# One more PSUM snapshot a unit, the output product one and a half units late, turned tiles fetched a phase ahead, norms and splits dealt out by a plan

## The chip, the cores and the metric

The kernel runs on one core of one Trainium2 chip. The metric is device time of one execution in microseconds (us), lower is better. TensorE (PE) multiplies matrices into PSUM; VectorE (DVE), ScalarE (ACT) and GpSimd (POOL) do elementwise work; SyncE (SP) issues all DMAs of this kernel. Each engine runs its own instructions in the order in which they are written.

## The reference

```python
scores = (1/S) * z @ z.T                  # per batch: B = 4, S = 3008, d_qk = 64
out    = u * (relu(scores) ** 2 @ v)      # v, u: 3008 x 256
x      = out.reshape(12032, 256)
xn     = x / sqrt(mean(x * x, -1) + 1e-6) * rms_g
g, val = xn @ w_gate, xn @ w_val          # 256 x 1536 each
result = (g * sigmoid(g) * val) @ w_out   # 1536 x 256
```

## The kernel before

Everything is kept transposed (features on partitions, tokens on columns). Each float32 matrix is split into a high and a low part, and a product is made of three matmuls (high by high, low by high, high by low).

The tokens are worked on in twelve pairs p of two column blocks of 512 (480 in every third pair), three pairs to a batch of 3008. Stage A(p) is attention for pair p: 24 steps ("slots") over key blocks of 128. A step takes scores (`emit_s`, PE lines 352 and 353, then ACT relu, line 357, and a DVE product, 359), splits them (`emit_l`: ACT 375, DVE 378, and ACT 395 or DVE 393 where a copy, "halves", is kept in DRAM), and multiplies them with v (`emit_av`: PE 417, 418, 422). Scores are symmetric, so some tiles are not computed again but fetched turned from those copies (`load_turned`, tile T). After the last step `emit_gate` (440) multiplies with u.

Stage M(p) is the feed-forward part: twelve units f of 128 hidden features (`Unit.run`). A unit forms its two 2x2 block products by Winograd's scheme, with seven products (A11, A12, S1, S2, S3, A22, S4; PE 597 to 599) into three PSUM tiles X, Z and V. X grows by five products; ACT copies it out in between (603: the snapshots s1, s2, s3), and DVE combines: 673 (Z + s1), 689 (V + s3), 692 (X * s1), 645 (V + s2), 652 (s2 * s3), with two Silus on ACT (682, 649). The two results of a unit are split (ACT 608 high, DVE 613 low: hH, hL) and multiplied with w_out (`y(0)`, `y(1)`: PE 624, 625, 628). In line 689 V is read in PSUM before its last product S4 is added, so S4 follows 689.

The stages stand in the order A0, A1, M0, A2, M1, ... A11, M10, M11. At the end of an M stage `tail` finishes its last unit while the next A stage enters. Four PSUM banks serve X, Z, V and the score tiles in rotation.

A table `jobs` holds side work at (stage, slot): `hook(phase, slot)` runs it in place. A unit has three slots: 3f behind y(0), 3f+1 behind y(1), 3f+2 ahead of A22. Side work is the norm of the next pair (`norm_jobs`: squares, sums, a 32x32 transpose, a fold matmul, an inverse root in small steps, scaling, four differences), the splits of keys (`prep_stat`) and of v (`prep_v`) for the next batch in M1, M4 and M7, the splits of the next queries (`prep_mov`, mh and ml), and in A0, A1 and M0 the decoding of the weights. `spread` deals it evenly over slots.

Of the kernel before, what the change touches and what calls it, by code (L numbers as in the profile page):

```python
# [19 lines left out]
P = 128  # L20
CH = 512
# [9 lines left out]
def kernel(  # L31
# [197 lines left out]
    raws = {True: ["raw", "xl4", "raw", "xl5", "xl6"], False: ["raw"]}  # L229

    def new_raw(first):
        ring = raws[first]
        ring.append(ring.pop(0))
        t = ring[-1]
        return (work if t == "raw" else moving).tile([P, CH], F32, tag=t, name="raw", bufs=2 if t == "raw" else 1)

    def prep_mov(p, k):
# [5 lines left out]
        def load():  # L243
            raw = tiles["raw"] = new_raw(p == 0)
            nc.sync.dma_start(out=raw[:, :n], in_=zT2[:, t0 + k * CH:t0 + k * CH + n])
# [12 lines left out]
    def prep_stat(b, c, shared=None):  # L258
# [6 lines left out]
        def load():  # L265
            raw = tiles["raw"] = new_raw(b == 0)
# [4 lines left out]
        def split():  # L271
            raw = tiles["raw"]
            z = keep.tile([P, CH], F32R, tag=f"zst{c}", name=f"zst{c}")
            nc.scalar.copy(z[:, :m], raw[:, :m])
            nc.vector.tensor_tensor(z[lo, :m], raw[lo, :m], f32(z[lo, :m]), op=ALU.subtract)
            zst[b, c] = z

        return load, split

    def prep_v(b, g):  # L280
# [4 lines left out]
        def load():  # L285
            view = tiles["raw"] = new_raw(b == 0).rearrange("p (a d) -> p a d", a=2)
# [7 lines left out]
        def split():  # L294
            hi = vh[b, g] = keep.tile([P, 2, D], F32R, tag=f"vh{g}", name=f"vh{g}")
            nc.scalar.copy(hi, tiles["raw"])
            lo = vl[b, g] = keep.tile([P, 2, D], F32R, tag=f"vl{g}", name=f"vl{g}")
            nc.vector.tensor_tensor(lo, tiles["raw"], f32(hi), op=ALU.subtract)

        return load, split  # L300
# [249 lines left out]
    def split_jobs(p):  # L550
# [3 lines left out]
        def one(o):  # L554
            def go():
# [8 lines left out]
                nc.vector.tensor_tensor(lo[:, :n], val, f32(hi[:, :n]), op=ALU.subtract)  # L564
                xsplit[p, o] = (hi, lo)
            return go
# [5 lines left out]
    units = {}  # L572

# [14 lines left out]
    class Unit:  # L588
# [12 lines left out]
        def snap(self, ps):  # L601
            s = work.tile([P, CH], F32, tag="r", name="s", bufs=6)[:, :self.n]
            nc.scalar.copy(s, ps[:, :self.n])  # L603
# [47 lines left out]
        def end2(self):  # L651
            nc.vector.tensor_tensor(self.s2, self.s2, self.s3, op=ALU.mult)

        def end3(self):
            self.high(1, self.s2)

        def end4(self):
            self.low(1, self.s2)

        def run(self, phase, prev, fill_a, fill_b):  # L660
# [10 lines left out]
            if prev:  # L671
                prev.end2()
            nc.vector.tensor_tensor(self.s1, Z[:, :n], self.s1, op=ALU.add)
            if prev:
                prev.end3()
# [12 lines left out]
            hook(phase, 3 * f + 1)  # L688
            nc.vector.tensor_tensor(self.s3, V[:, :n], self.s3, op=ALU.add)  # L689
# [4 lines left out]
            if f + ahead(self.p) < NF:  # L694
                load_unit(self.p, f + ahead(self.p))

        def tail(self, fills):

            fills = iter(fills)

            def fill():
                fn = next(fills, None)
                if fn:
                    fn()

            self.end0()
            fill()
            self.end1()
            self.end2()
            self.end3()  # L710
            self.y(0)
            fill()
            self.end4()
            self.y(1)

    def phase_a(p):

        ph = ("A", p)
        for i in range(NK):
# [5 lines left out]
            if i < NK - 1:  # L725
                for k in range(2):
                    emit_av(p, i, k)

    def rest_a(p):
        def one(k):  # L730
# [4 lines left out]
        return one(0), one(1)  # L735
# [4 lines left out]
    def phase_m(p, prev, fills):  # L740
        ph = ("M", p)
        for f in range(NF):
            u = Unit(p, f)
            if f == 0 and fills:
                a, b = fills
            else:
                a, b = (lambda u=prev: u.y(0)), (lambda u=prev: u.y(1))
            u.run(ph, prev, a, b)
# [5 lines left out]
    def spread(phase, slots, fns):  # L754
        slots = list(slots)
        for i, fn in enumerate(fns):
            at(phase, slots[min(i * len(slots) // len(fns), len(slots) - 1)], fn)

    def plan_batch(b):

        phase = ("M", b * NP - 2)
        todo = [prep_stat(b, c) for c in range(NC)] + [prep_v(b, g) for g in range(NK // 2)]
        return phase, todo

    for p in range(NPAIR):
        b, c0 = where(p)[:2]
        ph = ("A", p)
        if p:

            before = ("M", p - 2) if p > 1 else ("A", 0)  # L770
            for k in range(2):
                load, split, _ = prep_mov(p, k)
                if p > 1:
                    at(before, 3 * 9 + 2, load)
                    at(before, 3 * 10 + k, split)
                else:
                    at(before, NK - 4, load)
                    at(before, NK - 1, split)
        if p == 1:
            spread(ph, range(1, 18), [lambda i=i: deque(norms(0)[i]() or (), maxlen=0) and None for i in range(23)])  # L780
        if p:
            jl = [lambda i=i, p=p: splits(p - 1)[i]() for i in range(NO)]
            spread(ph, range(19, 23) if p == 1 else range(0, 7), jl)
        at(ph, 1 if p == 0 else (23 if p == 1 else 9), lambda p=p: load_u(p))
        for i in range(0, NK, 2):
            for k in range(2):
                if is_turned(p, i, k):
                    at(ph, max(i - 6, 0), lambda p=p, i=i, k=k: load_turned(p, i, k))
        for f in range(ahead(p - 1)):
            if p:  # L790
                at(ph, NK - 3 + f, lambda p=p, f=f: load_unit(p - 1, f))
        m = ("M", p - 1)
        if p:
            spread(m, range(1, 28) if p < NPAIR - 1 else range(1, 24), [lambda p=p, i=i: norms(p)[i]() for i in range(23)])
        if p == NPAIR - 1:
            spread(m, range(24, 36), [lambda p=p, i=i: splits(p)[i]() for i in range(NO)])
# [11 lines left out]

    for b in range(1, batch):
        phase, todo = plan_batch(b)  # L810
        n = len(todo)
        for k, (load, split) in enumerate(todo):
            s = 1 + 30 * k // n
            at(phase, max(s - 3, 0), load)
            at(phase, s + 1, split)
# [9 lines left out]
    for c in range(2, NC):  # L825
        s = 4 * c - 4
        at(("A", 0), s - 3, first["z", c][0])
        at(("A", 0), s, first["z", c][1])
    for g in range(2, NK // 2):
        s = 2 * g - 2  # L830
        at(("A", 0), max(s - 2, 0), first["v", g][0])
        at(("A", 0), s, first["v", g][1])
# [33 lines left out]
    with tc.manual_schedule():  # L866
# [6 lines left out]
        for c in range(2):  # L873
            first["z", c][1]()
            first["m", c][1]()
            if c == 0:
                first["v", 0][1]()
        emit_s(0, 0)
        first["v", 1][1]()
        emit_s(0, 1)  # L880
        emit_l(0, 0)
        phase_a(0)

        for go in rest_a(0):
            go()
        for go in enter_a(1):
            go()
        phase_a(1)
        fills = rest_a(1)
        prev = None  # L890
        for p in range(NPAIR):
            prev = phase_m(p, prev if not fills else None, fills)
# [43 lines left out]
```

## Time and profile before

| | |
|---|---|
| time, median of 3 runs | 2234.55 us (2229.3 to 2235.33) |
| time of the profiled execution | 2229.75 us |
| span of the profiled execution | 2228.0 us |
| PE busy | 2087.1 us (94%) |
| DVE busy | 1643.3 us (74%) |
| ACT busy | 1366.8 us (61%) |
| POOL busy | 129.1 us (6%) |
| mean granted TensorE clock | 0.978 |

The time is taken around the execution, the span from its first to its last instruction. A busy PE holds overlapping matmuls: the 512 column matmul is listed with about 390 ns, but the next one starts 227 ns later.

### The profile page before, as it was taken

How to read it: one execution, taken by the hardware profiler on the slowest of the kernel's cores; microseconds unless marked ns; L12 is line 12 of the kernel's file. 1: busy time of each engine (PE TensorE's matmuls, PEld its weight loads, DVE VectorE, ACT ScalarE, POOL GpSimd, SP SyncE). 2: the span in 40 equal slices, each digit the busy share in tenths (PEclk: the TensorE clock that was granted, in tenths of full speed). 3: DMA queues.
4: the chain of work that ended last, by engine and by line, in shares of the span. 5: the costliest groups of instructions: out<-in, count | busy, mean ns of one | idle time of the engine just before them, and what ended most of it. 6: DMA issues, size and time to landing. Idle time of an engine off the chain costs nothing. (4 is left out here: it accounts for less than half of the span.)

```text
span 2228.0 us, 26491 instructions
## 1 busy us (share of the span) xinstructions
PE 2087.1 (94%) x8968; PEld 1687.8 (76%) x8968; DVE 1643.3 (74%) x2697; ACT 1366.8 (61%) x2429; POOL 129.1 (6%) x232
## 2 busy tenths in 40 slices
PE   8988789998999999998999999999899999999998
PEld 6767567766887877876778777786688877878887
DVE  8988857686877677577778658758787866875865
ACT  7777447555855855555775675645586567564554
POOL 0635520000000000000000000000000000000000
PEclk9999989999999999999999999999999999999999
DMA  3405533242532742944253553394335355366342
GB/s 129 147 5 158 160 111 103 79 151 78 190 133 92 184 138 85 206 148 141 95 184 126 127 170 116 105 208 148 101 147 161 109 141 163 125 132 163 118 149 86
DMA packets 306825, 295.81 MB, mean 133 GB/s; under 512 B 195200, under 2 KB 232192, under 8 KB 306688
## 3 DMA queue, kind: packets, MB, share of 16 engines
q1 hardware_dynamic: 306688, 294.12, 43.9%
q8 instruction: 70, 1.15, 0.2%
q14 instruction: 67, 0.55, 0.1%
HBM read 178.46 MB, written 69.47 MB: 111 GB/s over the span
## 5 line engine op out<-in xcount | busy, mean ns | idle before, releaser
L597 PE MATMUL ps<-xh,wu 128*128 128x512 f32 (+1 forms) x1008 | 406.7, 404 | 61.0 <-DVE s L689 51.2
L417 PE MATMUL po<-H,vh 128*128 128x512 f32 (+1 forms) x1152 | 453.3, 394 | 9.2 <-ACT H L375 5.6
L418 PE MATMUL po<-H,vl 128*128 128x512 f32 (+1 forms) x1152 | 450.3, 391 | 0.0
L608 ACT CAST hH<-s 128x512 fp32r<-128x512 f32 (+1 forms) x288 | 176.4, 612 | 440.7 <-DVE s L692 324.7
L598 PE MATMUL ps<-xh,wu 128*128 128x512 f32 (+1 forms) x1008 | 394.2, 391 | 3.2 <-DMA wu<-wc 3.2
L599 PE MATMUL ps<-xl,wu 128*128 128x512 f32 (+1 forms) x1008 | 393.6, 391 | 0.0
L603 ACT COPY s<-ps 128x512 f32<-128x512 f32 (+1 forms) x432 | 248.6, 575 | 155.1 <-PE ps L599 147.0
L422 PE MATMUL po<-L,vh 128*128 128x512 f32 (+1 forms) x1104 | 340.6, 390 | 1.6 <-DVE L L378 1.3
L359 DVE TENSOR_TENSOR r<-ps,r 128x512 f32<-128x512 f32 x356 | 230.8, 680 | 123.0 <-ACT r L357 122.7
L597 PEld LDWEIGHTS ps<-xh,wu 128*128 128x128 f32 x1008 | 191.7, 190 | 147.6 <-DVE s L689 75.2
L357 ACT ACTIVATE r<-ps 128x512 f32<-128x512 f32 (+1 forms) x392 | 215.9, 599 | 133.8 <-PE ps L353 121.2
L378 DVE TENSOR_TENSOR L<-r,H 128x512 fp32r<-128x512 f32 x368 | 252.7, 697 | 49.4 <-ACT H L375 43.2
L417 PEld LDWEIGHTS po<-H,vh 128*128 128x128 f32 x1152 | 220.8, 192 | 59.0 <-ACT H L375 10.0
L418 PEld LDWEIGHTS po<-H,vl 128*128 128x128 f32 x1152 | 220.6, 192 | 41.9
L422 PEld LDWEIGHTS po<-L,vh 128*128 128x128 f32 x1104 | 209.2, 190 | 45.2 <-DVE L L378 5.3
L624 PE MATMUL py<-hH,woh 128*128 128x512 f32 (+1 forms) x576 | 224.7, 390 | 1.1 <-ACT hH L608 1.1
L628 PE MATMUL py<-hL,woh 128*128 128x512 f32 (+1 forms) x576 | 181.1, 396 | 46.0 <-DVE hL L613 46.0
L625 PE MATMUL py<-hH,wol 128*128 128x512 f32 (+1 forms) x576 | 223.2, 388 | 0.0
L599 PEld LDWEIGHTS ps<-xl,wu 128*128 128x128 f32 x1008 | 191.8, 190 | 38.4
L375 ACT CAST H<-r 128x512 fp32r<-128x512 f32 x356 | 217.8, 628 | 0.9 <-DVE r L359 0.9
L598 PEld LDWEIGHTS ps<-xh,wu 128*128 128x128 f32 x1008 | 192.1, 191 | 33.1 <-DMA wu<-wc 4.2
L613 DVE TENSOR_TENSOR hL<-s,hH 128x512 fp32r<-128x512 f32 (+1 forms) x288 | 196.4, 682 | 24.1 <-ACT hH L608 8.4
(80 smaller groups left out, 2635.8 us busy)
## 6 DMA issues: line engine op xcount, KB each, us to landing
wu<-wc SPq DMA_DIRECT2D x288, 448.0 KB, 4.0
kept<-halves SPq DMA_DIRECT2D x168, 256.0 KB, 2.0
raw<-in_v SPq DMA_DIRECT2D x44, 256.0 KB, 2.7
raw<-in_zT SPq DMA_DIRECT2D x38, 256.0 KB, 3.9
ux<-in_uT SPq DMA_DIRECT2D x16, 512.0 KB, 4.7
out_T<-y SPq DMA_DIRECT2D x32, 256.0 KB, 2.0
wc<-wohi SPq DMA_DIRECT2D x21, 256.0 KB, 2.5
wc<-wolo SPq DMA_DIRECT2D x21, 256.0 KB, 2.3
```

The source lines that it names most:

```text
L359: nc.vector.tensor_tensor(a[:, :n], ps[:, :n], a[:, :n], op=ALU.mult)
L375: nc.scalar.copy(hi[:, :n], a[:, :n])
L378: nc.vector.tensor_tensor(lo[:, :n], a[:, :n], f32(hi[:, :n]), op=ALU.subtract)
L417: nc.tensor.matmul(po[d][:, :n], wh[:, j, ds], hi[:, :n], start=(i == 0), stop=False)
L418: nc.tensor.matmul(po[d][:, :n], wl[:, j, ds], hi[:, :n], start=False, stop=(ends and lo is None))
L422: nc.tensor.matmul(po[d][:, :n], wh[:, j, ds], lo[:, :n], start=False, stop=ends)
L597: nc.tensor.matmul(ps[:, :n], wh[:, o, :], xh[:, :n], start=start, stop=False, skip_group_check=True)
L598: nc.tensor.matmul(ps[:, :n], wl[:, o, :], xh[:, :n], start=False, stop=False, skip_group_check=True)
L599: nc.tensor.matmul(ps[:, :n], wh[:, o, :], xl[:, :n], start=False, stop=stop, skip_group_check=True)
L603: nc.scalar.copy(s, ps[:, :self.n])
L624: nc.tensor.matmul(acc[h, d][:, :n], woh[:, f, ds], hi[:, :n], start=(f == 0), stop=False)
L625: nc.tensor.matmul(acc[h, d][:, :n], wol[:, f, ds], hi[:, :n], start=False, stop=False)
```

## The change

In each unit, ACT copies V into a fourth snapshot s4 right after S1 and S2, and the sum of line 689 is taken from s3 and s4, both in SBUF; S4 then no longer follows that sum. The output products are kept in a queue `pend`, from which a unit takes two: y(0) of a unit is issued in the second place of the next unit, y(1) in the first place of the one after. The last one and a half steps of attention go through the same queue. The tail issues three output products instead of two, and the split of the second result (`end3`) stands behind `emit_s(1)` and `emit_l(0)` without the copies of y(0) between.

Side work is dealt by `Beside.put`: each job has an engine and a cost, each slot has room (DVE 0.75 in every slot, ACT 1.35 in each third slot 3f+2), and a job goes to the first slot with room. Splits are parted into their ACT half (`one`) and their DVE half (`two`). The v splits of the later batches have their low part on POOL, in four pieces of 128 columns. The raw tiles of these batches take six buffers in turn: two named raw, and mh0, ml0, mh1, ml1, which are also the buffers of the next queries. Turned tiles of steps 4 to 7 are fetched in the last two units of the M stage before.

```diff
+    raws = {
+        "start": ["raw", "xl4", "raw", "xl5", "xl6"],
+        "batch": ["raw", "mh0", "raw", "ml0", "mh1", "ml1"],
+        "queries": ["raw"],
+    }
...
+        def one():
             hi = vh[b, g] = keep.tile([P, 2, D], F32R, tag=f"vh{g}", name=f"vh{g}")
             nc.scalar.copy(hi, tiles["raw"])
+        def two():
...
+            for a in range(2):
+                for k in range(0, D, PIECE):
+                    c = slice(k, k + PIECE)
+                    nc.gpsimd.tensor_tensor(lo[:, a, c], tiles["raw"][:, a, c], f32(hi[:, a, c]), op=ALU.subtract)
...
-        def run(self, phase, prev, fill_a, fill_b):
+        def run(self, phase, prev):
...
             self.product(X, S2, False, False)
+            s4 = self.snap(V, later=True)
             self.s2 = self.snap(X)
             if prev:
-                prev.end4()
-            nc.scalar.activation(self.s1, self.s1, AF.Silu)
-            fill_a()
+                prev.end2()
+            nc.scalar.copy(s4, V[:, :n])
             hook(phase, 3 * f)
+            if prev:
+                prev.end3()
+            pend.popleft()()
             self.product(X, S3, False, False)
             self.s3 = self.snap(X)
-            fill_b()
+            nc.scalar.activation(self.s1, self.s1, AF.Silu)
             hook(phase, 3 * f + 1)
-            nc.vector.tensor_tensor(self.s3, V[:, :n], self.s3, op=ALU.add)
+            nc.vector.tensor_tensor(self.s3, self.s3, s4, op=ALU.add)
+            pend.popleft()()
             hook(phase, 3 * f + 2)
...
+            pend.extend([lambda: self.y(0), lambda: self.y(1)])
...
+    for i, (e, cost, gap, fn) in enumerate(norm_plan(0)):
+        at(("A", 1), 1 + i * 17 // 23 + (2 if i >= 8 else 0) - (1 if i < 8 else 0), fn)
...
+                at(m.phase, 3 * 9 + 1 + k, load)
+                at(m.phase, 3 * 10 + 2 + k, split)
```

Three places show what the order becomes. In stage A1, on PE, the fold matmul of the first norm stands before the products of one key block (vh_126 and vh_215 are the v tiles of two key blocks that follow each other). Before:

```order
L352 MATMUL ps<-mh,zst_108 128x512
L353 MATMUL ps<-ml,zst_108 128x512
L480 MATMUL ps<-misc,fold_sb 128x32
L417 MATMUL po<-H,vh_126 128x512
L418 MATMUL po<-H,vl_128 128x512
```

and now:

```order
L366 MATMUL ps<-mh,zst_108 128x512
L367 MATMUL ps<-ml,zst_108 128x512
L494 MATMUL ps<-misc,fold_sb 128x32
L431 MATMUL po<-H,vh_215 128x512
L432 MATMUL po<-H,vl_250 128x512
```

It moved two steps later on PE; the DVE sum that it reads (474, now 488) stands one slot earlier.

In the tail from M6 to A8, on DVE, from the sum V + s2 of the last unit to the copies of its output (line 645 is now 665, 613 is 633, 378 is 392). Before:

```order
L645 TENSOR_TENSOR s<-ps,s 128x512
L359 TENSOR_TENSOR r<-ps,r 128x512
L359 TENSOR_TENSOR r<-ps,r 128x448
L613 TENSOR_TENSOR hL<-s,hH 128x512
L652 TENSOR_TENSOR s<-s 128x512
L636 COPY y<-py 128x512
L359 TENSOR_TENSOR r<-ps,r 128x512
L359 TENSOR_TENSOR r<-ps,r 128x448
L378 TENSOR_TENSOR L<-r,H 128x512
L378 TENSOR_TENSOR L<-r,H 128x448
L613 TENSOR_TENSOR hL<-s,hH 128x512
L636 COPY y<-py 128x512
```

and now:

```order
L665 TENSOR_TENSOR s<-ps,s 128x512
L373 TENSOR_TENSOR r<-ps,r 128x512
L373 TENSOR_TENSOR r<-ps,r 128x448
L633 TENSOR_TENSOR hL<-s,hH 128x512
L672 TENSOR_TENSOR s<-s 128x512
L373 TENSOR_TENSOR r<-ps,r 128x512
L373 TENSOR_TENSOR r<-ps,r 128x448
L392 TENSOR_TENSOR L<-r,H 128x512
L392 TENSOR_TENSOR L<-r,H 128x448
L633 TENSOR_TENSOR hL<-s,hH 128x512
L656 COPY y<-py 128x512 x2
```

The first copy of an output went behind the second hL; the second hL still follows both L.

At the end of M1 (M4 and M7 alike), on DVE, with the second block of the next queries. Raw tile 4727 is the v block 11; it, and ml_4879, lie in the buffer ml1. Before:

```order
L250 TENSOR_SCALAR mh_4775<-raw_4709 128x512
L251 SCALAR_TENSOR_TENSOR ml_4776<-raw_4709,mh_4775 128x512
L689 TENSOR_TENSOR s_4767<-ps_4738,s_4767 128x512
L692 TENSOR_TENSOR s_4725<-ps_4718,s_4725 128x512
L645 TENSOR_TENSOR s_4745<-ps_4738,s_4745 128x512
```

and now (the first block, into mh0 and ml0, stands one unit earlier, right ahead of that unit's L710):

```order
L254 TENSOR_SCALAR mh_4878<-raw_4745 128x512
L255 SCALAR_TENSOR_TENSOR ml_4879<-raw_4745,mh_4878 128x512
L633 TENSOR_TENSOR hL_4882<-s_4779,hH_4863 128x512
L545 TENSOR_TENSOR xc_4896<-ux1_3612,xc_4866 128x480
L706 TENSOR_TENSOR s_4893<-s_4893,s_4859 128x512
L545 TENSOR_TENSOR ux0_3610<-ux1_3612,ux0_3610 128x480
L545 TENSOR_TENSOR xc_4906<-ux1_3612,xc_4896 128x480
L710 TENSOR_TENSOR s_4842<-ps_4835,s_4842 128x512
```

while POOL's queue ends with the v blocks 9, 10 and 11, whose raw tiles lie in ml0, mh1 and ml1:

```order
L312 TENSOR_TENSOR vl7_4787<-raw_4547,vh7_4741 128x128 x4
L312 TENSOR_TENSOR vl8_4792<-raw_4549,vh8_4743 128x128 x4
L312 TENSOR_TENSOR vl9_4868<-raw_4637,vh9_4820 128x128 x4
L312 TENSOR_TENSOR vl10_4873<-raw_4639,vh10_4822 128x128 x4
L312 TENSOR_TENSOR vl11_4910<-raw_4727,vh11_4908 128x128 x4
```

The query splits, which waited for their own load, now also stand behind POOL's reading of these tiles; block 11 is copied by ACT in the last slot of the stage.

## Rows read from the trace of the kernel before

**Rows 1.** Waits of PE over the span: us in total, times, longest.

```profile
PE ps L597 <- DVE s L689: 51.2, 45, 3.4
PE py L628 <- DVE hL L613: 46.0, 20, 3.5
PE ps L480 <- issue: 6.8, 1, 6.8
```

**Rows 2.** Waits of PE within M0 alone (204 to 332 us).

```profile
PE ps L597 <- DVE s L689: 14.8, 8, 2.9
```

**Rows 3.** Windows M0, M3, A8, M7: us; busy PE, PEld, DVE, ACT, POOL; clock; DMA.

```profile
204.00:332.00 128.00, 102.75 (x398) 78.49 (x397) 92.85 (x155) 57.68 (x103) 47.73 (x92) 0.89 0.44 140
792.00:884.00 92.00, 90.93 (x400) 73.81 (x399) 71.06 (x118) 48.26 (x86) 0.00 (x0) 1.00 0.29 99
1425.00:1498.00 73.00, 68.51 (x307) 58.28 (x306) 44.82 (x73) 41.66 (x76) 0.00 (x0) 0.98 0.87 193
1498.00:1606.00 108.00, 98.41 (x402) 73.89 (x401) 79.92 (x135) 56.57 (x103) 0.00 (x0) 0.98 0.39 130
```

**Rows 4.** Timeline of PE in the tail of M6: start, us, [idle before].

```profile
1424.72 0.39 PE L352 MATMUL ps<-mh,zst 128*128 128x512 f32 x1
1424.95 0.39 PE L353 MATMUL ps<-ml,zst 128*128 128x512 f32 x1
...
1427.99 0.73 PE L628 MATMUL py<-hL,woh 128*128 128x512 f32 x2 [1.15 <-DVE hL L613]
...
1433.84 0.73 PE L628 MATMUL py<-hL,woh 128*128 128x512 f32 x2 [3.33 <-DVE hL L613]
```

**Rows 5.** Timeline of ACT in the same tail.

```profile
1428.58 0.62 ACT L608 CAST hH<-s 128x512 fp32r<-128x512 f32 x1 [1.54 <-DVE s L652]
1429.10 0.58 ACT L634 COPY y<-py 128x512 f32<-128x512 f32 x1
...
1431.00 1.06 ACT L395 COPY halves<-r 128x1024 uint16<-128x1024 uint16 x1
1431.94 0.58 ACT L375 CAST H<-r 128x448 fp32r<-128x448 f32 x1
```

**Rows 6.** Timeline of DVE in the same tail.

```profile
1424.24 0.69 DVE L692 TENSOR_TENSOR s<-ps,s 128x512 f32<-128x512 f32 x1 [0.68 <-PE ps L599]
...
1433.10 0.68 DVE L613 TENSOR_TENSOR hL<-s,hH 128x512 fp32r<-128x512 f32 x1
```

**Rows 7.** End of M7: DVE, then PE.

```profile
1594.40 0.43 DVE L250 TENSOR_SCALAR mh<-raw 128x512 fp32r<-128x512 f32 x1 [2.05 <-DMA raw<-in_zT]
...
1596.21 0.80 PE L597 MATMUL ps<-xh,wu 128*128 128x512 f32 x1 [3.17 <-DVE s L689]
```

**Rows 8.** The first fold in A1: PE, then DVE.

```profile
136.19 0.60 PE L480 MATMUL ps<-misc,fold_sb 128*128 128x32 f32 x2 [6.84 <-issue]
...
135.41 0.67 DVE L474 TENSOR_REDUCE misc<-q 128x16 f32<-128x512 f32 x1
```

**Rows 9.** DVE at the end of A1, and POOL there and in M0.

```profile
190.22 1.83 DVE L564 TENSOR_TENSOR xl<-ux,xh 128x512 fp32r<-128x512 f32 x2
194.55 1.28 DVE L564 TENSOR_TENSOR xl<-xc,xh 128x512 fp32r<-128x512 f32 x2
...
188.37 3.13 POOL L124 TENSOR_TENSOR wolo<-w,wohi 128x128 fp32r<-128x128 f32 x4
275.25 1.69 POOL L124 TENSOR_TENSOR ws<-w,w 128x128 f32<-128x128 f32 x4
```

**Rows 10.** Windows after a stall: the tail of M6, and M0 at 262.8 us.

```profile
1436.00:1440.00 4.00, 4.00 (x14) 3.31 (x13) 2.75 (x5) 2.53 (x5) 0.00 (x0) 0.66 0.63 212
...
262.00:266.00 4.00, 3.23 (x14) 2.68 (x15) 3.74 (x7) 1.64 (x3) 3.92 (x8) 1.00 0.44 131
```

**Rows 11.** First unit of M7 on PE, and a small norm step on DVE.

```profile
1506.14 0.50 PE L597 MATMUL ps<-xh,wu 128*128 128x512 f32 x1 [0.95 <-DVE s L689]
...
1539.62 0.18 DVE L490 TENSOR_TENSOR misc<-misc 128x30 f32<-128x30 f32 x1
```

More of the change, by code (lines that the diff above doesn't have):

```diff
@@ L265, in load @@
         def load():
-            raw = tiles["raw"] = new_raw(b == 0)
+            raw = tiles["raw"] = new_raw("batch" if b else "start")
             nc.sync.dma_start(out=raw[:, :n], in_=zT2[:, b * S + t0:b * S + t0 + n])
@@ L269, in load @@
                 nc.sync.dma_start(out=raw[:, n:m], in_=zT2[:, (b + 1) * S - TAIL:(b + 1) * S])
[L271 to L274, printed above, removed]
+        def one():
+            z = zst[b, c] = keep.tile([P, CH], F32R, tag=f"zst{c}", name=f"zst{c}")
+            nc.scalar.copy(z[:, :m], tiles["raw"][:, :m])
+        def two():
+            raw, z = tiles["raw"], zst[b, c]
             nc.vector.tensor_tensor(z[lo, :m], raw[lo, :m], f32(z[lo, :m]), op=ALU.subtract)
-            zst[b, c] = z
-        return load, split
+        return load, one, two
     def prep_v(b, g):
@@ L285, in load @@
         def load():
-            view = tiles["raw"] = new_raw(b == 0).rearrange("p (a d) -> p a d", a=2)
+            view = tiles["raw"] = new_raw("batch" if b else "start").rearrange("p (a d) -> p a d", a=2)
             if k0 + 2 < NK:
@@ L554, in one, with high @@
         def one(o):
-            def go():
+            def high():
                 val = xsplit[p, "values"][o]
@@ L724, in phase_a, with last @@
             hook(ph, i)
[L725 to L730, printed above, removed]
+            if i < NK - 2:
+                emit_av(p, i, 0)
+                emit_av(p, i, 1)
+            elif i == NK - 2:
+                emit_av(p, i, 0)
+        def last(k):
             def go():
@@ L749, in phase_m @@
             prev = u
         return prev
[L754 to L796, printed above, removed]
@@ new lines @@
+    beside = {}
+    for p in range(NPAIR):
+        b, c0 = where(p)[:2]
+        ph = ("A", p)
+        m = beside[p] = Beside(p)
+        for i in range(0, NK, 2):
+            for k in range(2):
+                if is_turned(p, i, k):
+                    go = lambda p=p, i=i, k=k: load_turned(p, i, k)
+                    if i < 8 and p > 1:
+                        at(("M", p - 2), 3 * (NF - 2 if i < 6 else NF - 1) + 1, go)
+                    else:
+                        at(ph, max(i - 7, 0), go)
+        if p:
+            for f in range(ahead(p - 1)):
+                at(ph, NK - 3 + f, lambda p=p, f=f: load_unit(p - 1, f))
+        at(ph, 1 if p == 0 else (23 if p == 1 else 10), lambda p=p: load_u(p))
+        if 0 < p < NPAIR:
+            for i in range(NO):
+                s = 19 + i * 4 // NO if p == 1 else i
+                one = lambda p=p, i=i: splits(p - 1)[i][0]()
+                two = lambda p=p, i=i: splits(p - 1)[i][1]()
+                at(ph, s, one)
+                at(ph, s + 1 if s < NK - 1 else s, two)
@@ new lines, in plan_batch @@
+    def plan_batch(b):
+        m = beside[b * NP - 2]
+        todo = [prep_stat(b, c) for c in range(NC)] + [prep_v(b, g) for g in range(NK // 2)]
+        done = []
+        for k, (load, one, two) in enumerate(todo):
+            if k == NC:
+                m.put(norm_plan(b * NP - 1), 1)
+            s = max(3 * (k // 2) - 2, 0) + k % 2
+            if k >= 6:
+                s = max(s, done[k - 6])
+            at(m.phase, s, load)
+            dve = k < NC
+            h = m.put([("a", 0.6, 0, one), ("d", 0.7 if dve else 0.0, 0, two)], s + 2)
+            done.append(h if dve else h + 1)
@@ L818 @@
+    for p in range(1, NPAIR):
+        for k in range(2):
+            load, split, _ = prep_mov(p, k)
+            if p > 1:
+                m = beside[p - 2]
+                at(m.phase, 3 * 9 + 1 + k, load)
+                at(m.phase, 3 * 10 + 2 + k, split)
+            else:
+                at(("A", 0), NK - 4, load)
+                at(("A", 0), NK - 1, split)
     first = {}
```

135 lines of the change are left out of this document (85 added, 50 removed).

## The prediction, made before the changed kernel ran

> **What bounds the kernel now.** I read the busy shares first, then the waits of PE, then the stages one by one. PE is busy 94% of a span of 2228.0 us, so what can be won is what PE waits, and what it loses at half clock after waiting. The waits name two lines: S4 behind the DVE sum of line 689, 51.2 us in 45 waits, and the output product behind hL, 46.0 us in 20 [rows 1]. A third is one wait of 6.8 us for the fold matmul [rows 1].
>
> By stage the first kind is uneven. M3, with nothing but a norm beside it, takes 92 us for 33 matmuls a unit; M7, which also splits keys and v for the next batch, takes 108 [rows 3], and so do M1 and M4. M0 takes 128, with 14.8 us of such waits [rows 2, 3]. The second kind sits in the tails: each of the ten has two stops, of 1.15 and 3.33 us in the one shown [rows 4]. A matmul of 512 columns starts 0.23 us after the one before (1424.72 to 1424.95) [rows 4]; I use 0.227, so a unit is 33 x 0.227 = 7.5 us. Neighbouring DVE operations start 0.60 us apart (two take 1.28 with the last one's 0.68) [rows 9], ACT copies about 0.5 (1428.58 to 1429.10) [rows 5].
>
> **The change, part by part.**
>
> *The fourth snapshot and the freed S4.* One more ACT copy a unit, 144 x 0.5 = 72 us of ACT. In M3 ACT is busy 48 of 92 us [rows 3]; with 12 x 0.5 it is 54. Between the end of S2 and the end of S3 lie nine matmuls, 2.0 us, in which ACT now has s2's copy, hH and s4: 1.5 us. It fits, with 0.5 us left: nothing. What the freed S4 brings is less than the 51.2 us, since the same late DVE is met one step further: the sum of line 692 frees X's bank, which the second product of the next unit needs six matmuls (1.36 us) after A22. In a first unit the two gates of 1.2 us stand ahead of 692 and end 0.5 us after A22; 692 ends at 1.2, just in time, so the wait of 0.95 us there [rows 11] goes. But the plan puts the 13 small norm steps of inverse root into two slots; they start about 0.22 us apart (0.18 busy [rows 11]), 2.9 us in one unit, and bring 692 about 0.5 us too late. For the eight plain M stages (all but M0, M1, M4, M7): 8 x (0.5 - 0.95) = -3 us; bounds 0 and -9.
>
> *M0.* DVE, ACT and POOL decode weights beside it, DVE works 92.85 of 128 us [rows 3], 7.7 us a unit where PE needs 7.5, and in between it waits for ACT and POOL: DVE sets the pace of these units, and freeing S4 doesn't shorten DVE. I take -4 us; bounds +4 and the 14.8 of [rows 2].
>
> *The fold.* In A1 PE stands at the fold until 136.19 us for a sum that DVE ends at 136.08 [rows 8]. A slot there is 16 matmuls, 3.6 us. The sum moves one slot earlier and the fold two later: 10.9 us against a wait of 6.84, so it goes. DVE is then about 1 us behind PE in the next products, which takes that back; and some 12 matmuls behind the stop ran at half clock, 12 x 0.2 = 2.4 us. -8 us; bounds 0 and -10.
>
> *The tail.* Its last output product needs the second hL, which DVE does behind both L of the first score tiles, and those wait for ACT. Between hH (1428.58) and the second H (1431.94) ACT did a copy of y, 0.5 us [rows 5]; it moves behind. So hL starts at 1432.6 instead of 1433.10 [rows 6], and PE goes on at 1433.36 instead of 1433.84 [rows 4]. The rest of the chain stays: it is now one stop of about 3.3 us. But six more matmuls of output product (1.36 us), taken from the M stage, are done inside it. 10 x (0.48 + 1.36) = -18 us; bounds -8 (only part of these six fall into the stop) and -46, all of [rows 1]. After the stop of 3.33 us the clock stood at 0.66 of full speed [rows 10], partly at the 1.2 GHz level; behind a shorter stop in M0, where PE is still busy 3.23 of 4 us, it stayed at 1.00 [rows 10]. One stop of 3.3 us is near the former, so I keep most of the loss (0.02 x 73 = 1.5 us a tail [rows 3]): -4 us of 15.
>
> *M1, M4, M7.* The v splits leave DVE: 12 x 0.6 = 7 us of 79.92 busy [rows 3]. On POOL four pieces take 1.69 us where little runs beside them and 3.13 where DVE runs [rows 9]; 12 blocks are 20 to 38 us, and POOL does nothing else there. The stops of M7, also the 3.17 us behind a late load [rows 7], have their cause removed: loads are earlier, ACT halves one slot ahead. That would make these stages 92 us. But a new wait comes: the query splits write the buffers ml0 and ml1 that POOL reads last. Count from the end of A22 in the tenth of the twelve units (t = 0). In the eleventh, S3 ends at 5.4, and ACT copies block 9 behind s3 and Silu, done at t = 7.1; POOL has read it at 9.1; DVE splits until 9.8 and ends 710 (the former 692) at 10.5. PE needs X's bank at 7.5 + 1.36 = 8.84: a stop of 1.7 us. Block 11 is copied in the last slot, 1.6 us after the end of the last unit's S3; POOL is through at 3.6; then DVE has ml, hL, three differences, s3 + s4 and 710, 7 x 0.6: X is free 7.9 us after S3. Queued on PE behind y, A22, S4 and one score tile (3.2 us) is the second score tile, which takes X's bank: a stop of 4.7 us, and the tail's own stop follows. With 2 us of half clock and 1 for the ports (below), 9.5 us of the 16 come back: 3 x -6.5 = -20 us; bounds -48 (no such wait) and +9.
>
> *Ports.* The 1.83 us for two DVE operations while POOL ran (188.37 to 191.5), against 1.28 with POOL done [rows 9], is 0.27 us more for each. 48 pieces x 0.27 = 13 us of DVE in M7: 80 - 7 + 13 = 86, still under 92. If a piece instead held DVE for its whole 0.7 us: 48 x 0.7 = 34, and 107 is over 92; DVE would set the pace. That is the second rival. The Trainium skill, page "SBUF — State Buffer", section "Who interferes with whom", says that a DVE instruction with two SBUF inputs and a POOL instruction that reads SBUF exclude each other, the second one waiting out the first. By that rule the v splits, and the sum s3 + s4 that no longer reads PSUM, work against this change; the rows here agree in kind, and show less than a whole piece for each operation.
>
> *At no cost:* the turned tiles fetched earlier. the large waits of PE [rows 1] name none of them, so what they shorten is ACT's idle time, behind PE's matmuls of the same step (16 x 0.227 = 3.6 us); without that cover, a step would be longer by what ACT waits beyond it.
>
> **The sum.** -3 - 4 - 8 - 18 - 4 - 20 = -57: a span of 2171 us. The profiled execution took 1.75 us more than its span, and the median of the runs shown is 4.8 above it; I add the 1.75 and half of the rest: **2175 us**.
>
> **Rivals.**
> 1. *The POOL reads end in time.* If ACT reaches blocks 9 and 11 early and the query splits wait for nothing, M1, M4 and M7 fall to 92 us: 3 x 9.5 = 28 less, 2147. For it: POOL is idle elsewhere, and ACT has slack. Against: block 11 stands in the last slot, behind ACT's own wait for S3.
> 2. *DVE and POOL exclude each other wholly.* The three stages stay near 107 and keep the two new stops: +9 a stage over my case, 2175 + 28 = 2203. For it the stretched rows; against it their size.
> 3. *Slower: the fourth copy makes snapshots late.* ACT stands between two products of X: the copy of s4 comes ahead of s3's, and both behind hH, which waits for DVE. If DVE is late by over 0.5 us in every unit, A22 waits by the rest. 144 units x 0.5 us = 72 more than my case: 2247. It decides from 0.4 us a unit on. Against it: in M3 PE has a wait in its first unit alone, and DVE is busy 71 of 92 us [rows 3].
>
> **How the numbers follow.** My case 0.60, rival 1 0.17, rival 2 0.17, rival 3 0.04, and 0.02 that little changes. My case alone is 2150 to 2195. The range from 2138 to 2208 takes in both rivals and leaves out about 2 in 10, with tails that lose all their stops below, and M stages with lasting new waits above. About 0.3% (6.7 us) is what a measurement here can tell from no change: faster 0.93, same 0.03, slower 0.04.
>
> **What would show it.** Right: no wait of PE at S4 for a DVE sum; one stop of some 3 us in each tail, before the last hL product; no wait at the fold; in M1, M4 and M7 a DVE line 255 that waits for POOL, with PE stops of about 2 and 5 us behind it, stages near 100 us; M3 at 91 to 92. Wrong: a score tile that waits for nothing at the end of M7, tails without a stop or with two, or PE waits for ACT's snapshots in plain units.

## The result, and the profile after

The changed kernel takes 2170.75 us (median of 4 runs, 2167.49 to 2173.18; forecast 2175) against 2234.94 for the kernel before in the same session: ratio 0.9715, 95% interval 0.9691 to 0.9738. The profiled execution has a span of 2171.4 us at a mean clock of 0.980; before it was 2228.0 at 0.978.

The busy line of the page of the changed kernel:

```profile
PE 2066.8 (95%) x8968; PEld 1696.4 (78%) x8968; DVE 1614.9 (74%) x2661; ACT 1433.0 (66%) x2573; POOL 207.9 (10%) x376
```

144 more ACT copies make 66 us more of ACT, and 144 small pieces 79 us more of POOL. Waits of PE over the span (us, times, longest):

```profile
PE py L648 <- DVE hL L633: 31.2, 13, 3.1
PE ps L616 <- DVE s L710: 19.8, 12, 4.9
PE ps L616 <- DMA wu<-wc: 12.3, 2, 8.0
...
PE ps L366 <- DVE s L710: 4.9, 3, 1.6
...
PE ps L617 <- DMA wu<-wc: 3.6, 2, 2.0
PE ps L367 <- DVE ml L255: 3.0, 4, 0.9
```

Against [rows 1]: the 51.2 us at S4 are now 19.8 behind the product of line 710 (the former 692), 13 of them in M0; the output product (L648) waits 31.2 in 13 waits instead of 46.0 in 20; the wait at the fold is gone. The waits for weight tiles (wu), all in M0, grew from 9.7 to 15.9. New are waits of score tiles at the ends of M1, M4 and M7, 4.9 us and 2.7 of the 3.0. The stages as in [rows 3] (us; busy PE, PEld, DVE, ACT, POOL; clock; DMA), M0, M3, A8, M7:

```profile
197.00:335.00 138.00, 107.40 (x401) 82.04 (x400) 99.02 (x162) 64.97 (x120) 52.12 (x92) 0.87 0.41 133
781.00:872.00 91.00, 90.83 (x401) 74.55 (x400) 68.68 (x118) 53.35 (x97) 0.00 (x0) 1.00 0.43 124
1392.00:1465.00 73.00, 70.09 (x313) 59.33 (x312) 45.15 (x73) 42.54 (x77) 0.00 (x0) 0.98 0.79 166
1464.00:1558.00 94.00, 91.40 (x402) 74.62 (x401) 70.29 (x116) 62.25 (x115) 23.87 (x47) 1.00 0.45 149
```

M7 fell from 108 to 94 us. M0 did not fall: it went from 128 to 138. Below, a stage M reaches from its first product (line 616) to its last, and an A stage, with the tail ahead of it, lies between two of them. Summed so over the two profiled executions (us):

| part | forecast | measured |
|---|---|---|
| plain M stages, 8 | -3 | -11.0 |
| M0 | -4 | +9.2 (128.7 to 137.9) |
| A0 and A1 with the fold | -8 | -6.9 (203.9 to 197.0) |
| M1, M4, M7, each with the A stage behind it | -20 and 3 of 10 tails (-6.7) | -36.9 (600.7 to 563.8) |
| the seven other tails | -15.7 | -11.2 |
| span | -57 | -56.6 |

That the total was met so closely is in part luck: 18 us too little were expected in the plain M stages (8) and in M1, M4 and M7 with the A stages behind them (10), and 19 too much in M0 (13), in the other tails (4.5) and at the fold (1).

A plain tail, that of M6 in the changed kernel: PE from the first score tile on, then DVE, then ACT ([rows 4 to 6] before).

```profile
1391.68 0.39 PE L366 MATMUL ps<-mh,zst 128*128 128x512 f32 x1
...
1400.38 1.22 PE L648 MATMUL py<-hL,woh 128*128 128x512 f32 x2 [2.91 <-DVE hL L633]
...
1399.10 0.63 DVE L392 TENSOR_TENSOR L<-r,H 128x448 fp32r<-128x448 f32 x1 [0.53 <-ACT H L389]
1399.64 0.68 DVE L633 TENSOR_TENSOR hL<-s,hH 128x512 fp32r<-128x512 f32 x1
...
1395.61 0.62 ACT L628 CAST hH<-s 128x512 fp32r<-128x512 f32 x1 [1.53 <-DVE s L672]
1398.50 0.57 ACT L389 CAST H<-r 128x448 fp32r<-128x448 f32 x1
```

One stop is left of two. From the first score tile to the last output product it is 8.70 us (before 9.12): the chain is 0.42 us shorter, and the output product that fills it is 1.36 us longer. hL (DVE 1399.64) starts 4 us after its high half (ACT 1395.61), because both L of a score tile stand ahead of it.

The end of M7: DVE, PE, POOL.

```profile
1549.32 0.93 DVE L255 SCALAR_TENSOR_TENSOR ml<-raw,mh 128x512 fp32r<-128x512 f32 x1 [1.19 <-POOL vl L312]
1558.60 0.69 DVE L255 SCALAR_TENSOR_TENSOR ml<-raw,mh 128x512 fp32r<-128x512 f32 x1 [4.26 <-POOL vl L312]
1562.11 0.68 DVE L710 TENSOR_TENSOR s<-ps,s 128x512 f32<-128x512 f32 x1
...
1550.90 0.50 PE L616 MATMUL ps<-xh,wu 128*128 128x512 f32 x1 [1.30 <-DVE s L710]
1559.34 0.50 PE L367 MATMUL ps<-ml,zst 128*128 128x512 f32 x1 [0.89 <-DVE ml L255]
1562.85 0.50 PE L366 MATMUL ps<-mh,zst 128*128 128x512 f32 x1 [1.63 <-DVE s L710]
...
1547.32 4.07 POOL L312 TENSOR_TENSOR vl<-raw,vh 128x128 fp32r<-128x128 f32 x8 [2.77 <-ACT vh L301]
1556.85 1.71 POOL L312 TENSOR_TENSOR vl<-raw,vh 128x128 fp32r<-128x128 f32 x4 [5.46 <-ACT vh L301]
```

The two forecast waits of the query splits for POOL are there, 1.19 and 4.26 us of DVE. The first gives PE a stop of 1.30 us (forecast 1.7), the second stops of 0.89 and 1.63 (forecast 4.7 in one).

### The profile page after: what moved, and what is told of

The parts are those of the page before. It is cut to its first block, busy times and chain, and to the rows that moved or that the text cites. A ratio compares the mean times of both kernels' runs of the same rounds, so it can differ in the third digit from the quotient of the medians.

```text
span 2171.4 us, 27099 instructions
## 1 busy us (share of the span) xinstructions
PE 2066.8 (95%) x8968; PEld 1696.4 (78%) x8968; DVE 1614.9 (74%) x2661; ACT 1433.0 (66%) x2573; POOL 207.9 (10%) x376
## 4 chain that ended last, share of the span: by engine, by line
PE 78%; issue 7%; DVE 7%; ACT 4%; POOL 4%; DMA 2%; POOLq 0%; DVEq 0%; SPq 0%; ACTq 0%
PE po L431 11%; PE po L432 11%; PE po L436 11%; PE ps L616 8%; PE ps L618 8%; PE ps L617 8%; PE py L648 4%; PE py L644 4%; PE py L645 4%; PE ps L367 4%; PE ps L366 4%; POOL vl L312 3%; DVE hL L633 1%; ACT r L371 1%; DVE L L392 1%
## 5 line engine op out<-in xcount | busy, mean ns | idle before, releaser
L616 PE MATMUL ps<-xh,wu 128*128 128x512 f32 (+1 forms) x1008 | 398.0, 395 | 36.0 <-DVE s L710 19.8
L617 PE MATMUL ps<-xh,wu 128*128 128x512 f32 (+1 forms) x1008 | 392.3, 389 | 3.6 <-DMA wu<-wc 3.6
L648 PE MATMUL py<-hL,woh 128*128 128x512 f32 (+1 forms) x576 | 180.1, 394 | 31.2 <-DVE hL L633 31.2
```

Of the source, the lines that this page charges most:

```text
L616: nc.tensor.matmul(ps[:, :n], wh[:, o, :], xh[:, :n], start=start, stop=False, skip_group_check=True)
L617: nc.tensor.matmul(ps[:, :n], wl[:, o, :], xh[:, :n], start=False, stop=False, skip_group_check=True)
L648: nc.tensor.matmul(acc[h, d][:, :n], woh[:, f, ds], lo[:, :n], start=False, stop=(f == NF - 1))
```

## The experiments

Each kernel is the changed one with one edit, if nothing else is said; ratios are to the kernel before on the same chip. That kernel took 2229.9 to 2234.9 us on the chips used, so a difference in us between runs on two chips can carry some 5 us of that; lengths of stages are read from the profiled executions.

**1. The fourth snapshot alone**, in the kernel before.

```diff
...
             self.product(X, S2, False, False)
+            s4 = self.snap(V, later=True)
             self.s2 = self.snap(X)
             if prev:
                 prev.end4()
+            nc.scalar.copy(s4, V[:, :n])
...
-            nc.vector.tensor_tensor(self.s3, V[:, :n], self.s3, op=ALU.add)
+            nc.vector.tensor_tensor(self.s3, self.s3, s4, op=ALU.add)
```

> The kernel before with one part alone: V is copied into a fourth snapshot and line 689 sums the two copies; the queue of output products, the plan and the buffers stay as before. My theory: a late DVE is what stops PE, and freeing S4 moves the stop to the second product of the next unit, where it is shorter by at most 1.36 us a unit. So the waits of PE at S4 (51.2 us) come back as 25 to 40 us of waits behind the sum of line 692, and the time falls by 10 to 25 us, to 2210 to 2225. Rival: the sum in PSUM itself was the obstacle, and nearly all 51 us go: 2180 to 2190.

Measured: 2224.6 us, ratio 0.9973 (0.9955 to 0.9991), some 6 us. That is less than expected, and the rival's 51 are far off. Its waits in M0 (here line 695 is the product of X and s1):

```profile
PE ps L597 <- DMA wu<-wc: 10.8, 2, 5.5
PE ps L597 <- DVE s L695: 4.2, 5, 1.9
PE ps L598 <- DMA wu<-wc: 3.8, 3, 1.7
PE ps L597 <- ACT s L604: 2.9, 10, 1.1
```

Against [rows 2] the wait for DVE fell from 14.8 to 4.2, and most of it came back as waits for weight tiles and for snapshots: M0 went from 128.7 to 125.9. M1 stayed at 108.1, M3 went from 92.0 to 91.9.

**2. The turned tiles fetched late again.**

```diff
-                    if i < 8 and p > 1:
-                        at(("M", p - 2), 3 * (NF - 2 if i < 6 else NF - 1) + 1, go)
-                    else:
-                        at(ph, max(i - 7, 0), go)
+                    at(ph, max(i - 6, 0), go)
```

> The changed kernel, with the turned tiles fetched as before (six steps ahead, none in the stage before). My theory: PE waits for none of them, so 2171 within 5 us. Rival: the early fetch carried part of the gain of the stages A4 to A11 (they fell by 0.5 to 4.4 us each), and the time rises by 8 us or more.

Measured: 2168.5 us, 0.9733 (0.97 to 0.9766): the early fetch is worth nothing that can be measured.

**3. Buffers of their own for the last three v blocks of a batch** (the three "out" buffers), so that the query splits find theirs free.

```diff
-        "batch": ["raw", "mh0", "raw", "ml0", "mh1", "ml1"],
+        "batch": ["raw", "mh0", "raw", "ml0", "mh1", "ml1"] * 2 + ["raw", "mh0", "raw", "out", "out", "out"],
...
```

> The changed kernel, with the last three v blocks of each later batch loaded into the three buffers named out, which the feed-forward stage leaves idle, so that the splits of the next queries have mh and ml to themselves. My theory: the DVE waits of 1.2 and 4.3 us for POOL at line 255 go, and with them PE stops of 1.5, 1.0 and 1.8 us and part of the half clock behind them, in three stages: 10 to 18 us less, 2153 to 2161. Rival: DVE would be late there anyway, from the small norm steps, the differences and the shared ports, and the time stays within 5 us of 2171.

Measured: 2160.64 us, 0.969 (0.9658 to 0.9722). The low halves of the queries wait for nothing now; DVE, then POOL:

```profile
1538.03 0.83 DVE L255 SCALAR_TENSOR_TENSOR ml<-raw,mh 128x512 fp32r<-128x512 f32 x1
1543.22 0.69 DVE L255 SCALAR_TENSOR_TENSOR ml<-raw,mh 128x512 fp32r<-128x512 f32 x1
...
1537.24 4.49 POOL L312 TENSOR_TENSOR vl<-raw,vh 128x128 fp32r<-128x128 f32 x8 [3.08 <-issue]
```

M7 with A9 went from 187.8 to 184.2 us; the three such pairs together lost 12. So the new waits are real, and cost some 10 us of the time (8 against run 2, on the same chip).

**4. The same, and the low halves of v on DVE.**

```diff
-            if b == 0:
+            if True:
...
-            dve = k < NC
+            dve = True
```

> The kernel with own buffers for the query splits (2160.6 us), and the low part of v on DVE again instead of POOL, dealt by the plan at 0.7 a block. POOL and DVE then share nothing in M1, M4 and M7, and DVE has 7 us more in each. If the shared ports cost as much as the work moved off DVE saved (my estimate: 13 us of stretched DVE against 7 saved), the time is 2154 to 2166. Rival: taking this work off DVE is what shortened these stages by 14 us each, and the time is 2175 or more.

Measured: 2160.44 us, 0.9686 (0.9663 to 0.9709), the same as run 3. DVE is busy 3 us more in M7 (76.3 of 91 instead of 73.0 of 92), and PE does not see it. POOL was not needed for these splits, nor did it hurt.

**5. The work of a batch dealt evenly**, with POOL and the six buffers kept.

```diff
-            s = max(3 * (k // 2) - 2, 0) + k % 2
...
-            h = m.put([("a", 0.6, 0, one), ("d", 0.7 if dve else 0.0, 0, two)], s + 2)
+            s = 1 + 30 * k // len(todo)
+            at(m.phase, max(s - 3, 0), load)
+            at(m.phase, s + 1, one)
+            at(m.phase, s + 1, two)
+        for i, (e, cost, gap, fn) in enumerate(norm_plan(b * NP - 1)):
+            at(m.phase, 1 + i * 27 // 23, fn)
```

The first square stands ahead of the gate of its column block here (in run 6 too): that part of the norm takes values not yet multiplied with u. No work is left out.

> The changed kernel, with the splits for the next batch and the norm in M1, M4 and M7 dealt evenly as before: ACT half and DVE half of a split in one slot, any slot; POOL and the six buffers stay. Theory: DVE waits in order for the ACT half, and ACT's halves stand ahead of the snapshots, so these stages grow from 93.7 to 97 to 103 us and the time to 2181 to 2199, less what the earlier last blocks save at the queries' split. Rival: the freed S4 and POOL brought the 14 us of these stages, and the dealing nothing: 2171 within 6 us.

Measured: 2170.72 us, 0.974 (0.971 to 0.9765). M7 is 3.7 us longer (97.4) and A9 3.6 shorter (90.5): the waits moved from the end into the middle of the stage, their sum stayed. The plan's table of costs, by itself, brings nothing there.

**6. The norm beside M0 dealt evenly.**

```diff
+        if p == 1:
+            for i, (e, cost, gap, fn) in enumerate(norm_plan(p)):
+                at(m.phase, 1 + i * 27 // 23, fn)
+            continue
         h = m.put(norm_plan(p), 1)
```

> The changed kernel, with the norm beside M0 dealt evenly over slots 1 to 27 as before, all else as changed. M0 became longer, 128.7 to 137.9 us, against my forecast. Theory: the plan packs that norm into slots 2 to 24, knows nothing of the weight decoding in the same slots, and so makes DVE late in the first units, and with it the weights of the last third: M0 falls back by 4 to 9 us and the time to 2162 to 2167. Rival: M0 only starts 7 us earlier and meets a chain of weights that ends when it did, whoever deals the norm: within 4 us of 2171.

Measured: 2163.81 us, 0.9705 (0.9679 to 0.9732). M0 took 132.2 us, with 8.4 us of waits behind line 710 instead of 13.0. Six kernels that share the changed kernel's M0 show 134.1 to 136.5 for it (runs 2 to 5, 7 and 8; the changed kernel itself 137.9), so the plan costs M0 some 3 us, hardly more than it varies by, and what is left over 128.7 has another cause.

**7. The first norm at its old slots** (the fold as before).

```diff
-        at(("A", 1), 1 + i * 17 // 23 + (2 if i >= 8 else 0) - (1 if i < 8 else 0), fn)
+        at(("A", 1), 1 + i * 17 // 23, fn)
```

> The changed kernel, with the first norm in A1 at the slots of before (the sum and the fold matmul in one slot). PE should stand at the fold again for 6 to 7 us, and A0 with A1 take 203 us instead of 197. If the chain of weights sets the end of M0 by itself, M0 gives that back (130 us instead of 138) and the time stays within 4 us of 2171. If not, M0 keeps its 138 us and the time is 2177 to 2180.

Measured: 2175.77 us, 0.9754 (0.973 to 0.978). The wait of 6.8 us at the fold is back, A0 and A1 take 204.4 instead of 197.0, and M0 is no shorter for it (135.6). So the fold's 7 us are real.

**8. The low half of the second result first** in the tail.

```diff
             self.end1()
             self.end2()
+            self.end3()
             pend.popleft()()
             if fills:
                 fills.popleft()()
-            self.end3()
```

> The changed kernel, with one line of the tail moved: the second low part (end3) stands directly behind the second high part, ahead of the second score tiles and both L. My theory: the one stop of 2.9 us that each of the ten tails has left comes from DVE's order alone (hL is ready to run 3.4 us before DVE gets to it), so the stop falls below 0.5 us and most of the half clock behind it goes: 25 to 40 us less, 2131 to 2146. Rival: the stop only moves to the first attention products, which then wait for L: less than 8 us.

Measured: 2146.05 us, 0.9628 (0.9594 to 0.9663), at a clock of 0.99. Its tail of M6 on PE:

```profile
1378.42 0.62 PE L648 MATMUL py<-hL,woh 128*128 128x512 f32 x2
...
1380.72 0.50 PE L431 MATMUL po<-H,vh 128*128 128x512 f32 x1 [0.82 <-ACT y L654]
...
1383.54 0.48 PE L431 MATMUL po<-H,vh 128*128 128x448 f32 x1 [0.40 <-DVE y L656]
```

The output product waits for nothing; instead the first products with v wait for the copies of y, 0.82 and 0.40 us. Four microseconds behind the stop, in the changed kernel and in this one:

```profile
1400.50:1404.50 4.00, 4.00 (x11) 3.26 (x12) 2.50 (x5) 2.44 (x5) 0.00 (x0) 0.59 0.67 259
```

```profile
1381.00:1385.00 4.00, 3.57 (x15) 2.30 (x15) 2.64 (x5) 3.17 (x6) 0.00 (x0) 1.00 0.74 285
```

Behind a stop of 2.91 us PE ran mostly at the 1.2 GHz level; behind 0.82 and 0.40 it stayed at 2.4 GHz. A8 went from 72.2 to 70.0 us, of which 1.7 are stops; the A stages from A4 on lost 1.1 to 3.7 us each. Less than 0.5 us of stops was expected to be left, and 1.2 is; the time lies at the upper end of what was expected.

**9. The output products at their old distance.**

```diff
-            if i < NK - 2:
+            if i < NK - 1:
                 emit_av(p, i, 0)
                 emit_av(p, i, 1)
-            elif i == NK - 2:
-                emit_av(p, i, 0)
...
-        pend.extend([lambda: emit_av(p, NK - 2, 1), last(0), last(1)])
+        pend.extend([last(0), last(1)])
...
```

> The changed kernel with the output products at their old distance: a unit issues y(0) and y(1) of the unit just before it, and only the last step of attention (not the last one and a half) goes through the queue, so that a tail has two output products left and not three. All else stays. Theory: six matmuls of output product, 1.36 us, leave each tail's stop, and the stop comes back as two: the A stages get longer by 1.4 to 2 us each, ten times, and the ends of M1, M4 and M7 lose the cover of y(1), 1.4 us more each. 2171 + 14 to 25 = 2185 to 2196. Rival: the tail is set by the chain DVE, ACT, DVE alone and the six matmuls fit elsewhere: within 5 us of 2171. M0 is open: at its old distance the output product may meet the late sums of DVE less often or more often; if the lateness is what made M0 longer by 9 us, it falls from 138 to about 130.

Measured: 2188.14 us, 0.98 (0.9774 to 0.9827). The tail of M6 has its two stops again:

```profile
1405.68 0.74 PE L648 MATMUL py<-hL,woh 128*128 128x512 f32 x2 [1.18 <-DVE hL L633]
1411.53 1.22 PE L648 MATMUL py<-hL,woh 128*128 128x512 f32 x2 [3.32 <-DVE hL L633]
```

and the ends of M1, M4 and M7 a wait of 4.0 us for hL each: these three pairs of stages take 11 us more, the six plain tails from A4 on 11 more, and M0 5 less (132.9). So the late output product gives 22 us there and takes 5 back in M0; the time shows 17 (19 by the ratios). The waits of PE within M0, first with the output products early, then in the changed kernel:

```profile
PE py L648 <- DVE hL L633: 10.8, 7, 2.5
PE ps L616 <- DMA wu<-wc: 6.6, 2, 4.1
PE ps L616 <- DVE s L710: 6.1, 3, 3.0
PE ps L617 <- DMA wu<-wc: 3.8, 2, 2.4
```

```profile
PE ps L616 <- DVE s L710: 13.0, 6, 4.9
PE ps L616 <- DMA wu<-wc: 12.3, 2, 8.0
```

The sum of waits is much the same, 29 and 31 us, but with the late product they come in fewer and longer pieces, up to 8.0 us. The clock over M0 is 0.92 of 133 us there, 0.87 of 138 here. At two levels that is 2 x 0.08 x 133 = 21 and 2 x 0.13 x 138 = 36 us at the lower one. Of the 5 us between the two, 1.7 are waits, and 3.3 are time in which PE is busy (104.2 and 107.5).

**10. Output products at their old distance, norm beside M0 even** (slots 2 to 27).

```diff
-        h = m.put(norm_plan(p), 1)
+        if p == 1:
+            for i, (e, cost, gap, fn) in enumerate(norm_plan(p)):
+                at(m.phase, max(2, 1 + i * 27 // 23), fn)
+            continue
+        h = m.put(norm_plan(p), 1)
```

> The kernel with the output products at their old distance, and the norm beside M0 dealt evenly over slots 2 to 27. It is for M0 alone, where the time went up: 128.7 us before, 125.9 with the fourth snapshot alone, 132.9 with all of the change but the late output product, 134 to 138 with it. Theory: what is left over the 125.9 is the plan, which puts the norm's DVE work into the first slots, where DVE also decodes weights: M0 comes to 126 to 129, the time to 2188 - 5 = 2183. Rival: M0 stays at 131 to 134 and the time at 2186 to 2190, since the wait for weight tiles and the half clock behind it, not the norm, set these units.

Measured: 2187.05 us, 0.9801 (0.9765 to 0.9838), M0 129.9: the stage lies between the two forecasts, the time in the rival's. The clock over M0 is 0.89, lower than in run 9 (0.92), though M0 is 3 us shorter. Without the late product and the plan's norm M0 is back near the 128.7 of before, though not at the 125.9 of run 1.

**11. Runs 3, 8 and the norm of run 10 together**, on the changed kernel.

> Three edits at once on the changed kernel: the low half of the tail's second result (end3) right behind end2, the last three v blocks of a batch in buffers of their own, and the norm beside M0 dealt evenly over slots 2 to 27 (no square stands ahead of the gate of its column block here). Theory that they add up: 2171 - 25 - 10 - 5 = about 2131 (2125 to 2138). Rival: two of them win the same half clock and the same stop at the ends of M1, M4 and M7, so that together they bring no more than the low half alone and M0's part, 2140 to 2146. In the trace A3, A6 and A9 should take about 89 us, M1, M4 and M7 92, M0 132.

Measured: 2128.54 us, 0.9538 (0.9517 to 0.9559): they add up, 42 us below the changed kernel. Its waits, and the end of M6 with A8 at full clock:

```profile
PE ps L616 <- DVE s L710: 12.3, 8, 4.6
PE ps L616 <- DMA wu<-wc: 10.5, 2, 6.8
PE po L431 <- ACT y L654: 8.7, 10, 0.9
```

```profile
1364.00:1434.00 70.00, 68.74 (x311) 57.53 (x310) 45.19 (x74) 42.17 (x76) 0.00 (x0) 1.00 0.76 173
```

A3, A6 and A9 take 88.1 us (94.3 in the changed kernel), M0 134.6, where 132 was expected; of the 68 us that PE still waits, 27 are in M0.

**12. Run 11 with the stores of the combined weights issued by POOL.**

```diff
-                    nc.sync.dma_start(
+                    nc.gpsimd.dma_start(
```

> As the run before it, and the stores of the combined weights (line 198, wc) are issued by POOL, behind its own pieces, not by SP. Theory: PE's waits in M0 for weight tiles (DMA wu, 16 us of M0) come from SP's queue, where loads stand behind stores that wait for POOL; without these stores in that queue the waits fall below 6 us, M0 goes from 132 to 122 to 126 us, and the time is 6 to 10 us less than that of the run before. Rival 1: the weight tiles are late because POOL's pieces are late and not because of the queue: the same waits, the same time within 2 us. Rival 2: POOL's own issuing holds its pieces up, and M0 gets longer by some us.

Measured: 2140.39 us, 0.9591 (0.957 to 0.9611), 12 us more. The second rival holds. Some of PE's waits, and POOL in A0:

```profile
PE ps L616 <- ACT s L623: 11.3, 19, 7.9
PE ps L366 <- DVE mh L254: 9.4, 2, 9.0
...
PE ps L616 <- DMA wu<-wc: 7.9, 1, 7.9
```

```profile
102.29 0.77 POOL L198 DMA_DIRECT2D wc<-wohi  x1
103.06 0.75 POOL L198 DMA_DIRECT2D wc<-wolo  x1
```

Two issues take 1.5 us of POOL for each combined block. The waits for weight tiles in M0 fall from 14.8 to 8.3 us, other waits take their place (M0 137.1), and A0 with A1 go from 197.6 to 206.9.

## Why the prediction was right, and where its parts were not

**The fourth snapshot.** As forecast: no wait at S4, little gained (run 1), and no stop for late snapshots in plain stages, so the slower rival is out. The term for plain stages, -3, was mis-sized: the wait of 0.95 us in first units went, but the 0.5 us for the small norm steps did not come: in M3 of the changed kernel PE waits 0.2 us in all, though the 13 steps stand in one unit (816.34 to 819.51 us) right ahead of its product 710 (819.62). Run 9, without the late product, has M3 at 90.7 us as well; so this comes neither from the snapshot alone nor from that product. Which part of the dealing, or of the new order within a unit, brings it was not tried apart.

**M0** is the step that failed, in sign. The prediction argued "DVE sets the pace of these units, and freeing S4 doesn't shorten DVE. I take -4 us". For the snapshot that was right (-2.8 in run 1). But it priced that edit alone there, and had no term for the weight tiles, for which PE already waited in M0 of the kernel before:

```profile
PE ps L597 <- DMA wu<-wc: 6.5, 2, 3.6
PE ps L598 <- DMA wu<-wc: 3.2, 2, 2.7
```

These 9.7 us became 14.6 with the snapshot alone and 15.9 with the whole change, while the waits for DVE went from 14.8 to 4.2 and to 13.0. Two edits lengthen M0. The plan puts the norm into the first free slots and knows nothing of the decoding that DVE does in the same slots (some 3 us by runs 6 and 10, less by run 11). The late output products remove 10.8 us of waits for hL (run 9), but these come back as waits for DVE (6.1 to 13.0) and for weight tiles (10.4 to 15.9); that costs 5 us by run 9, and 2 by runs 10 and 6, which differ alike. It is not that M0 starts 7 us earlier: in run 7 it starts as late as before, and PE waits 15.7 us for weight tiles there too. What makes these tiles late stays open: run 12, with the stores out of SP's queue, keeps one wait of 7.9 us for them (8.0 in the changed kernel), which points at the blocks that POOL decodes and not at that queue, but does not show it. That longer stops cost M0 more by a lower clock is not shown either: run 10 has the lower clock than run 9 and the shorter M0.

**The fold.** -8 forecast, -6.9 in the stages, and undone it gives 7.4 back (run 7), of which the time keeps some 5.

**The tails.** Right in mechanism: one stop, before the last hL product, with the chain 0.42 us shorter (forecast 0.48). The stops shrank by 1.6 us a tail (4.5 to 2.9), where 1.84 was forecast. That most of the half clock stays was right, and the 4 us of it that were forecast back did not come: seven tails lost 11.2 us, as much as their stops. Run 8 shows its price: with the stop gone, the time falls by 25 us (22 against run 2, on the same chip), more than the 16 us of stops that it removes, and the clock stays up.

**M1, M4, M7.** The waits of the query splits for POOL are as forecast, and the first stop nearly (1.3 us; its 7.5 + 1.36 is 8.86, not 8.84). The second was mis-sized: "the second score tile, which takes X's bank: a stop of 4.7 us". It is the third tile that takes it, behind y(1), whose six matmuls (1.36 us) cover part; and the second waits only for its own ml. 2.5 us in place of 4.7, three times, and no half clock inside the stages (clock 1.00 in M7). Without the late product, in run 9, the three pairs take 11 us more, of which some 5 are what three plain tails lose there too. The M stage itself shrank by 14. Some 5 of these are the late product (run 9, 98.9), and the rest comes neither from POOL (run 4) nor from the snapshot (run 1, 108.1). Nor does it come from the plan, from earlier slots of the loads or from halves in different slots: run 5 has the old slots for loads and splits, with both halves in one, and its three pairs take 562.9 us (563.8). What is left is the six buffers, and the new order within a unit; these two were not tried apart. In M7 of the kernel before, SP's loads of v and of keys waited 20.5 and 19.0 us for DVE's splits to free a buffer; in run 5 the longest such sum is 0.6 us.

**Ports.** The second rival is out: with the v splits on DVE the time is the same (run 4). The operation of line 255, which reads two SBUF tiles, is stretched beside POOL's pieces, 0.93 and 0.83 us against 0.69, and the slack of DVE takes that. The pieces of POOL around the operation of 1549.32, one by one, and the DVE operation behind it:

```profile
1549.24 0.45 POOL L312 TENSOR_TENSOR vl<-raw,vh 128x128 fp32r<-128x128 f32 x1
1549.66 0.90 POOL L312 TENSOR_TENSOR vl<-raw,vh 128x128 fp32r<-128x128 f32 x1
1550.53 0.45 POOL L312 TENSOR_TENSOR vl<-raw,vh 128x128 fp32r<-128x128 f32 x1
...
1550.17 0.68 DVE L710 TENSOR_TENSOR s<-ps,s 128x512 f32<-128x512 f32 x1
```

The piece at 1549.66, which met line 255, took twice as long; the next one and line 710, which has an input in PSUM, ran side by side and lost nothing. The Trainium skill, page "SBUF — State Buffer", section "Who interferes with whom", has a DVE operation with two SBUF inputs and a POOL operation that reads SBUF exclude each other; the trace agrees: the DVE operation, begun 0.4 us before the end of a piece, lost 0.24 us, and the piece behind it 0.45. The price was mis-sized: the prediction charged DVE 0.27 us for each of 48 pieces, 13 us a stage. M7 shows some 4: DVE is busy 73.0 us in run 3, and 76.3 in run 4, where 7.4 are the v splits. (The second rival's own price was not consistent either: 107 us and both stops are about 12 a stage more than the forecast, not 9.)

**Turned tiles.** Nothing, as forecast (run 2).

**The first rival**, that POOL ends in time, was wrong, since the waits came; but run 3 shows that freeing the buffers was worth some 10 us, not its 28.

## What to carry to other kernels

A sum that is met can still hide parts that cancel: check each stage against its own term, and price every edit in every stage that it reaches, not only in the one it is meant for. Removing the last link of a stop (here one DVE operation of 0.68 us that stood behind two others which nobody needed yet) brought 22 to 25 us, on top of the 17 that filling it with other work had brought; the first without the second was not tried. And a planner's costs mislead where they don't know all the work of the slot (M0, some 3 us).

## What was not expected of the hardware

- A DMA issue on POOL took 0.75 to 0.77 us of POOL (run 12), as much as one and a half pieces of its work; on SP, which does nothing else in this kernel, the same issues took 0.36 and 0.42 us (medians, changed kernel).
- The mean clock of a stage does not give its length: with the same matmuls, M0 took 133 us at 0.92 (run 9), 138 at 0.87 (changed kernel) and 130 at 0.89 (run 10).
- Ten tails with a stop of mostly 2.9 to 3.1 us left a mean clock of 0.98, but not each was followed by the lower level: A7, behind 3.1 us, kept 1.00 and took 81.8 us, where its likes A4 and A10 took 84.5 and 83.5. With stops of 0.8 and 0.4 no A stage behind A1 showed the lower level, and the mean clock was 0.99 (run 8).
